# A bank for products of ones, and the order of the first loads, in an attention and feed-forward block

## The chip, the cores and the metric

The kernel runs on one core of a Trainium2 chip. The metric is the device time of one execution in microseconds (us); the time before the change is the median of three runs.

## The reference

The input x has 2048 rows (tokens) of 512 numbers. Two branches are computed from it and joined:

```python
x = A_x
xn = _layernorm(x, axis=-1)
s = _A_ref(xn, A_wqkv, A_wo)           # sliding attention, 32 heads of 16, window 256
g = _silu(_B_ref(xn, B_w1, B_w3, B_w2))  # silu(xn @ w1) * (xn @ w3) @ w2, inner width 1792
return x + s * g
```

In `_A_ref` the queries, keys and values come from one product with `wqkv` (512 x 1536). A token sees itself and the 255 tokens before it; the softmax of the scaled scores weighs the values, and the result is multiplied by `wo`. All tensors are float32.

## The kernel before

**Number format.** Nearly every matrix product is made of three float16 products. An operand is scaled by a power of two and cut into a high float16 part and a low one (`split`: ScalarE casts the high part, VectorE subtracts it for the low part; `split_pool` leaves the subtraction to GpSimd). The scale comes from the norm of each weight: `squares` sums squares on ScalarE (L249) and VectorE (L251), the sums are cast to bf16 (L261), `powers` adds them over the partitions by a product with ones (L280, or L285 inside a bank of scores), and VectorE turns the sum into a power of two (L291 to L304).

**Tiling.** Tokens go in four tiles of 512 (t = 0 to 3), heads in four groups of eight (g), and the feed-forward width in 14 blocks of 128 (f). `project(t, g, k)` makes the queries (k = 0) or keys (k = 1) of one tile and group: it accumulates twelve products (L596) in one PSUM bank, ScalarE takes the high part out (L613), VectorE the low part (L617), and both are stored to DRAM (`dQ`, `dK`, L620 to L624). `fetch(t, g)` loads them back in another layout (L640, four DMAs). `value(j)` makes the values of 128 tokens (L566, taken out in L569). `pass1` computes scores for their row maxima (L664, L678), `negate` and `finish` prepare the maxima as extra rows of the queries (L690, L691, L697, then DMAs in L708), and `pass2` computes the scores again, their exponentials (L755) and the products with the values (L773). `gate_up(t, f)` is the feed-forward's first step (L1035), `down` and a later folded form its second (L1260, L1178).

**PSUM.** Two banks m0 and m1 are handed out in turn by `bank()`. Two double banks for scores are handed out in turn by `scores_bank()`. One more, `po`, belongs to the outputs of attention.

**Loads of weights.** `load(0, f)` loads block f of w1 and w3 (two DMAs, L867), `load_down(0, f)` block f of w2 (L912), `weights_qk(g)` the query and key weights of a group (two DMAs, L394), `weights` those of the values (L358). All go through SyncE's queue (SP). Each load notes its DMA in `lasts["load"]`; so does `fetch`. `measure(f)` takes the norms of blocks f and f + 1 of w1 and w3.

**Order.** The order of TensorE's instructions is the order in which the program writes them. The other engines' instructions, and SP's DMAs, are put in an order at compile time from estimated times and from priorities; `tc.issue_after(ins)` adds that what is written inside it stands behind `ins` on the same engine. It is an order only and makes no wait by itself. Each engine then works down its list. `behind_load()` is `issue_after` the last noted load. `later(n, f)` calls f after n more steps of the program, and a step follows each piece of dense work.

**The opening.** The program loads the first tile of x, the weights of groups 0 and 1, the values' weights, blocks 0 and 1, the weights of group 2 and blocks 2 and 3 (L1508 to L1524). TensorE meanwhile runs products of ones whose results nobody reads (`keep_busy`, L1533): 24 of them at the start, 3 behind the first norm, and 4 behind the transposes (L1560). Then come the projections of tile 0, group 0 (`k00`, `q00`, L1563), those of group 1, two parts of the values, and the first scores with values and feed-forward work spread between them. The first keys are projected in a scores bank, the first queries in an m bank.

Of the kernel before, what the change touches and what calls it, by code (L numbers as in the profile page):

```python
# [10 lines left out]
F32 = mybir.dt.float32  # L11
# [10 lines left out]
P = 128  # L22
# [9 lines left out]
TW = S // NT  # L32
# [30 lines left out]
LEAD = 5  # L63
# [20 lines left out]
def tile_block(ctx: ExitStack, tc: tile.TileContext, x, wqkv, wo, w1, w3, w2, out):  # L84
    nc = tc.nc
# [18 lines left out]
    pss = pool("pss", 2, PSUM)  # L104
# [39 lines left out]
    def later(n, f):  # L144
        made_so_far[0] += 1
        queue.append((now[0] + n, made_so_far[0], f))
# [16 lines left out]
    def bank(shape, dtype=F32):  # L163

        open_bank[0] = b = 1 - open_bank[0]
        return psm.tile(shape, dtype, name=f"m{b}", tag=f"m{b}", bufs=1)

    def scores_bank():

        return pss.tile([P, 2, 512], F32, name="s")  # L170
# [65 lines left out]
    def behind_load():  # L236

        return tc.issue_after(lasts["load"].ins) if "load" in lasts else nullcontext()
# [341 lines left out]
    def project(t, g, k, terms=(range(3),), scores_bank=False):  # L580


        cell = {}

        parts = ([[(c, i) for c in (2 * half, 2 * half + 1) for i in range(3)] for half in range(2)] if len(terms) == 1
                 else [[(c, i) for i in group for c in range(NC)] for group in terms])

        def part(n):
            assert turned[t] == 4
            w = WQ[t, g, k]  # L590
            xh, xl = X[t]
            if n == 0:
                cell["pp"] = pss.tile([P, 2, TW], F32, name="s")[:, 0, :] if scores_bank else bank([P, TW])
            for c, i in parts[n]:
                a, b = ((0, xh), (1, xh), (0, xl))[i]
                nc.tensor.matmul(cell["pp"], w[:, (a * NC + c) * P:(a * NC + c + 1) * P], b[:, c, :], start=(c, i) == parts[0][0],  # L596
                                 stop=(c, i) == parts[-1][-1])
            if n < len(parts) - 1:
                return
            if t == 0:  # L600
                def store():
                    with behind_load():
                        nc.sync.dma_start(dWQ[g, k], w)
                    give(w, after=8)
                later(45, store)
            else:
                give(w)
            pp = cell["pp"]
            both = take(F16)
            B = both.rearrange("p (a t) -> p a t", a=2)  # L610
            s = QS / (XS * WS)
            with urgent():
                nc.scalar.activation(B[:, 0, :], pp, AF.Copy, scale=s)  # L613

            def rest():
                with urgent():
                    lasts["emptied"] = nc.vector.scalar_tensor_tensor(B[:, 1, :], pp, s, B[:, 0, :], op0=ALU.mult, op1=ALU.subtract)  # L617
                d = (dQ, dK)[k][g][:, :, t * TW:(t + 1) * TW]
                if k == 0:
                    nc.sync.dma_start(d[:, 0:2, :], B[:, 0:1, :].to_broadcast([P, 2, TW]))  # L620
                    nc.sync.dma_start(d[:, 2, :], B[:, 1, :])
                else:
                    nc.sync.dma_start(d[:, 0:2, :], B)
                    nc.sync.dma_start(d[:, 2, :], B[:, 0, :])  # L624
                give(both, after=4)
            later(1, rest)
        return opening([(len(l), lambda n=n: part(n)) for n, l in enumerate(parts)])
# [230 lines left out]
    def load(t, f):  # L858
        if t:
            a = [take(F16) for _ in range(2)]  # L860
            WF[t, f] = [a, None]
            for k in range(2):
                lasts["load"] = nc.sync.dma_start(a[k], dW1[f, k])
            return
        RAW[f] = raw = [take(F32) for _ in range(2)]
        for k, w in enumerate((w1, w3)):
            lasts["load"] = nc.sync.dma_start(raw[k].rearrange("p (c f) -> p c f", f=P),  # L867
                              w[:, f * P:(f + 1) * P].rearrange("(c p) f -> p c f", p=P))

    measured = set()  # L870

    def measure(f, apart=0):
# [33 lines left out]
    def load_down(t, f):  # L906
        if t:
            WF[t, f][1] = b = take(F16)
            nc.sync.dma_start(b, dW2[f])
            return  # L910
        RAW2[f] = raw = take(F32)
        lasts["load"] = nc.sync.dma_start(raw, w2[f * P:(f + 1) * P, :])  # L912

    def measure_down(k, f):

# [438 lines left out]
    def feed_forward():  # L1354

        pieces = []
        late = []
        cuts_at = []
        for t in range(NT):
            for f in range(FB):  # L1360
                if t == 0:

                    if (f % 2 or f == 0) and f + LEAD < FB - 2:
                        pieces += [(0, lambda f=f: load(0, f)) for f in (range(f + LEAD, f + LEAD + 2) if f else range(4, LEAD + 1))]
                    elif f + LEAD == FB - 1:
                        pieces += [(0, lambda f=f: load(0, f)) for f in range(FB - 2, FB)]
                    if f % 2 and f + 3 < FB:
                        pieces.append((0, lambda f=f + 3: later(5, lambda: measure(f, 1)) if f == 6 else measure(f, 1)))
                    pieces += [(0, lambda f=f: load_down(0, f)) for f in range(f + 2 if f else 0, min(f + 3, FB))]
                    for m in range(f + 1 if f else 0, min(f + 2, FB)):  # L1370
                        k = next(k for k, (_, f1) in enumerate(GROUPS) if m < f1)
                        pieces.append((0, lambda k=k, m=m: later(2, lambda: measure_down(k, m))))
                else:
                    if f == 0:
                        pieces += [(0, lambda t=t, f=f: load(t, f)) for f in range(2)]
                    if f + 2 < FB:
                        pieces.append((0, lambda t=t, f=f + 2: load(t, f)))

                    if t == 1:
                        pieces.append((0, lambda t=t, f=f: load_down(t, f)))  # L1380
                    if t == 1 and f in FOLD_AT:
                        work = fold_weights(FOLD_AT.index(f))
                        pieces.append((0, work[0]))
                        cuts_at.append((f + 2, work))
                    for at, work in cuts_at:
                        if t == 1 and f == at:
                            pieces.append((0, work[1]))
                if f == FB - 4 and t + 2 < NT:
                    first, second = prepare_beside(t + 2, 8)
                    pieces += first  # L1390
                if f == 0 and t > 2:
                    pieces += soon
                made = gate_up(t, f)
                for at, work in cuts_at:
                    if t == 1 and f == at:
                        made.insert(2, (0, lambda work=work: later(6, work[2])))
                pieces += made
                pieces += late
                late = []
                if t < 2:  # L1400
                    for k, (f0, f1) in enumerate(GROUPS):
                        if f == f1 - 1:
                            late = [q for b in range(4) for q in down(t, k, b)]
                for k, (j0, j1) in enumerate(FOLDS):
                    if t > 1 and f == 2 * j1 - 1:
                        soon, late = folds(t, k)
                        if k == 0 or t == NT - 1:
                            pieces += soon
            if t + 2 < NT:
                pieces.append((0, second))  # L1410
        return pieces + late
# [85 lines left out]
    def run(dense):  # L1497
        for c, piece in dense:
            piece()
            if c:  # L1500
                step()
# [18 lines left out]
    load(0, 0)  # L1520
    load(0, 1)
    qk[2][0]()
    load(0, 2)
    load(0, 3)  # L1524

    for b in range(VB):
        nc.gpsimd.memset(V[:, b, 0:H * VW].rearrange("p (h w) -> p h w", w=VW)[:, :, DH:VW], 1.0)
# [2 lines left out]
        nc.gpsimd.memset(KA[2][:, a, :].bitcast(F32), TWO_ONES)  # L1530


    def keep_busy(n):  # L1533
        ps = bank([P, 4, P])
        for _ in range(n):
            nc.tensor.matmul(ps, onesb, onesb.unsqueeze(1).to_broadcast([P, 4, P]), start=True, stop=True)

# [19 lines left out]
        flush()  # L1557
    with tc.issue_after(lasts["hi"].ins), tc.issue_after(lasts["x"].ins):
        qk[1][1]()
    keep_busy(4)  # L1560


    k00, q00 = (project(0, 0, k, ((0,), (1,), (2,)), k) for k in (1, 0))  # L1563
    run([k00[0], q00[0], k00[1]])
    qk[1][2]()
    with tc.issue_after(lasts["scale"].ins):
# [3 lines left out]
    with tc.issue_after(lasts["hi"].ins):  # L1570
        run([k00[2], q00[2]])
    later(1, lambda: fetch(0, 0))
    k01 = project(0, 1, 1, ((0, 2), (1,)))
    run(k01[:1])
    wv[2]()
# [4 lines left out]
    sc["o"] = scaled(SQ["wv"][3], OS / WS, "so")  # L1580
    with tc.issue_after(lasts["hi"].ins):
        measure(0)
    run(project(0, 1, 0, scores_bank=True))
    later(1, lambda: fetch(0, 1))
    run(value(0, True))
    qk[2][1]()
    run(value(1))
    qk[3][0]()
    started.append(True)
    measure(2, 1)  # L1590
    beside_scores(4, lambda s: then(s, qk[2][2](s), lambda: later(1, qk[2][3])))
# [84 lines left out]
```

## Time and profile before

| what | value |
|---|---|
| median of three runs | 813.16 us (813.06 to 813.75) |
| the profiled execution | 813.03 us |
| its span, from the first to the last instruction | 811.2 us |
| TensorE busy | 794.5 us, 98% of the span |
| VectorE, ScalarE, GpSimd busy | 634.2, 392.5 and 364.0 us |
| granted TensorE clock | 1.000 |
| moved by DMA | 134.18 MB, mean 165 GB/s |

In the profile PE is TensorE, PEld its weight loads, DVE VectorE, ACT ScalarE, POOL GpSimd, and SPq stands for DMAs as SyncE issues them. A row of a timeline gives the start in us, the length in us, the engine, the line of the kernel, the operation, what it writes and reads, and how often; in square brackets stands how long the engine had been idle and what it waited for. A row of the waits gives who waited for whom, the total in us, how many times, and the longest. A row of the windows gives for a stretch of time the length, the busy time and count of each engine, the granted clock, the share of the time that the 16 DMA engines were busy, and GB/s.

### The profile page before, as it was taken

To read this page: it belongs to the slowest core of one execution; us is meant where nothing else is said; L and a number is where in the kernel's file an instruction comes from. 1 tells how busy PE (TensorE), PEld (TensorE's weight loads), DVE (VectorE), ACT (ScalarE), POOL (GpSimd) and SP (SyncE) were. 2 spreads that over 40 slices of the span, in tenths; PEclk is the share of its full clock that TensorE was granted. 3 is DMA by queue.
4 is the path that set the end of the run, shared out by engine and by line. 5 is a ranking of instruction groups with operands and counts; after the bars stand their busy time and mean duration, and the time that the engine had idled before them with its cause. 6 is when DMAs were issued, how large, how long until landed. Compare 5 with 4: busy or idle time off the path is not lost.

```text
span 811.2 us, 23867 instructions
## 1 busy us (share of the span) xinstructions
PE 794.5 (98%) x9176; PEld 404.2 (50%) x9176; DVE 634.2 (78%) x2037; ACT 392.5 (48%) x591; POOL 364.0 (45%) x648
## 2 busy tenths in 40 slices
PE   8999989999999999999999999999999999999998
PEld 4444444444544444444444454456544654466465
DVE  8788788887898777887988888777777887875437
ACT  6879586563536554445444434344444234344421
POOL 2234266232329546354354355530246277560670
PEclk9999999999999999999999999999999999999999
DMA  9978554835566375657655634656462544335321
GB/s 283 253 221 264 156 190 124 283 117 190 158 180 215 127 249 140 214 145 251 171 162 175 193 98 132 174 150 176 116 189 72 162 138 139 113 85 174 112 67 60
DMA packets 109794, 134.18 MB, mean 165 GB/s; under 512 B 18864, under 2 KB 64880, under 8 KB 109680
## 3 DMA queue, kind: packets, MB, share of 16 engines
q1 hardware_dynamic: 109392, 132.13, 54.7%
q8 instruction: 72, 1.18, 0.6%
q10 hardware_dynamic: 288, 0.52, 0.2%
q14 instruction: 42, 0.34, 0.1%
HBM read 91.23 MB, written 36.57 MB: 158 GB/s over the span
## 4 chain that ended last, share of the span: by engine, by line
PE 80%; DVE 9%; ACT 5%; issue 3%; DMA 2%; SPq 0%; DVEq 0%; POOL 0%; ACTq 0%
PE m L1035 30%; PE po L773 8%; PE m L1260 8%; PE m L1178 8%; PE m L596 7%; PE s L745 5%; PE m L1312 4%; PE m L566 4%; PE s L664 3%; DVE junk L678 2%; PE po L664 2%; ACT sqa L249 1%; ACT slot L342 1%; ACT pt L755 1%; DMA dW<-slot 1%
## 5 line engine op out<-in xcount | busy, mean ns | idle before, releaser
L1035 PE MATMUL m<-XH,slot 128*128 128x512 f16 x896 | 267.3, 380 | 1.6 <-DVE slot L617 1.2
L755 ACT ACTIVATE pt<-s,es 128x1024 f32<-128x1024 f32 x152 | 167.7, 1113 | 192.8 <-DVE s L752 174.6
L339 POOL TENSOR_TENSOR slot<-slot,slot 128x256 f16<-128x256 f32 (+1 forms) x170 | 113.2, 694 | 212.2 <-ACT slot L1068 85.0
L1035 PEld LDWEIGHTS <-slot 128*128 128x128 f16 x1344 | 124.8, 98 | 155.9 <-issue 12.4
L1035 PE MATMUL m<-XL,slot 128*128 128x512 f16 x448 | 169.8, 379 | 0.0
L752 DVE TENSOR_TENSOR s<-s,MK 128x256 f32<-128x256 f32 (+2 forms) x280 | 118.8, 435 | 50.7 <-PE s L745 46.4
L678 DVE CUSTOM_DVE_ANT_0 junk<-s,MW 128x320 bf16<-128x320 f32 x276 | 133.9, 485 | 18.0 <-PE s L664 10.3
L678 DVE CUSTOM_DVE_ANT_0 junk<-po,MW 128x320 bf16<-128x320 f32 x172 | 83.5, 485 | 4.3
L1260 PE MATMUL m<-slot,slot 128*128 128x512 f16 x336 | 78.6, 380 | 0.4 <-DVE slot L1054 0.4
L773 PE MATMUL po<-pt,V 64*32 64x320 f32 (+4 forms) x2880 | 77.2, 342 | 0.8 <-DVE pp L304 0.8
L596 PE MATMUL m<-XH,slot 128*128 128x512 f16 x240 | 70.9, 380 | 1.5 <-DVE slot L1054 0.8
L1178 PE MATMUL m<-slot,slot 128*128 128x256 f16 x588 | 68.4, 273 | 0.0
L1093 POOL TENSOR_TENSOR slot<-slot,slot 128x256 f16<-128x256 f32 x98 | 64.6, 671 | 1.1
L1050 ACT ACTIVATE slot<-m,sgs 128x512 f32<-128x512 f32 x56 | 38.3, 684 | 54.4 <-PE m L1035 53.0
L1178 PEld LDWEIGHTS <-slot 128*128 128x128 f16 x588 | 56.2, 98 | 11.4 <-issue 3.0
L773 PEld LDWEIGHTS po<-pt,V 64*32 64x32 f32 x2880 | 50.4, 106 | 23.0 <-PE s L514 0.9
L1054 DVE SCALAR_TENSOR_TENSOR slot<-slot,m 128x512 f32<-128x512 f32 x56 | 38.3, 684 | 27.9 <-ACT slot L1050 27.8
L745 PE MATMUL s<-qa,KA 50*64 50x320 f16 (+3 forms) x1472 | 58.3, 259 | 0.3 <-DVE M L678 0.2
L596 PEld LDWEIGHTS <-slot 128*128 128x128 f16 x384 | 35.6, 98 | 44.7 <-issue 3.3
L745 PEld LDWEIGHTS <-KA 50*64 50x64 f16 x1472 | 30.1, 105 | 52.1 <-issue 31.4
L1260 PEld LDWEIGHTS <-slot 128*128 128x128 f16 x336 | 30.7, 98 | 38.7 <-issue 4.3
L664 PE MATMUL s<-KA,qa 48*64 48x320 f16 (+3 forms) x824 | 45.0, 294 | 4.1 <-ACT pt L755 2.9
(188 smaller groups left out, 1096.9 us busy)
## 6 DMA issues: line engine op xcount, KB each, us to landing
slot<-dW SPq DMA_DIRECT2D x98, 256.0 KB
slot<-in_B_w_dram SPq DMA_DIRECT2D x56, 256.0 KB
slot<-dFold SPq DMA_DIRECT2D x48, 256.0 KB
dW<-slot SPq DMA_DIRECT2D x42, 256.0 KB
slot<-in_A_x_dram SPq DMA_DIRECT2D x30, 256.0 KB
KA<-dK SPq DMA_DIRECT2D x24, 288.0 KB
qa<-dQ SPq DMA_DIRECT2D x32, 192.0 KB
slot<-dWQ SPq DMA_DIRECT2D x24, 256.0 KB
```

Source lines behind the costliest of these rows:

```text
L339: op(out[:, c], a[:, c], b[:, c])
L596: nc.tensor.matmul(cell["pp"], w[:, (a * NC + c) * P:(a * NC + c + 1) * P], b[:, c, :], start=(c, i) == parts[0][0], stop=(c, i) == parts[ ...
L664: nc.tensor.matmul(s[c:c + w, r, :n], qa[rows, 2 * p + a, ii * P + c:ii * P + c + w], ka[rows, 2 * p + a, e - n:e], start=True, stop=True)
L678: lasts["maximum"] = nc.vector.tensor_tensor_reduce(out=junk[:, :n], in0=s[:, r, :n], in1=mask, scale=1.0, scalar=NEG, op0=ALU.add, op1=AL ...
L745: nc.tensor.matmul(s[64 * h:64 * h + 64, r, o:o + 64 * n], ka[rows, 2 * p + a, 64 * (m + 4):64 * (m + 5)], qa[rows, 2 * p + a, 64 * (m + k ...
L752: nc.vector.tensor_add(v, v, MK[:, kind, of:of + n, :].unsqueeze(1).to_broadcast([P, 2 * len(which), n, 64]))
L755: lasts["exp"] = nc.scalar.activation(pt, s, AF.Exp, scale=es)
L773: nc.tensor.matmul(cell["po"][32 * i:32 * i + 32, h, 64 * (m + k):64 * (m + k + n)], V[64 * h:64 * h + 64, (4 * t + m // 2) % VB, hd * VW: ...
L1035: nc.tensor.matmul(cell[k], w[:, (a * NC + c) * P:(a * NC + c + 1) * P], b[:, c, :], start=c == 0 and i == 0, stop=c == NC - 1 and i == 2)
L1093: nc.gpsimd.tensor_sub(lo, view, hi)
L1178: nc.tensor.matmul(cell["ps"][:, c], made[:, f:f + P], wj[:, g:g + 256], start=j == j0 and c == 0 and n == 0, stop=j == j1 - 1 and n == 2, ...
L1260: nc.tensor.matmul(ps, hh[:, a * TW + b * P:a * TW + (b + 1) * P], w[:, c * D:(c + 1) * D], start=f == f0 and i == 0, stop=f == f1 - 1 and ...
```

## The change

Three things are changed. The second group of products of ones is written to a scores bank, the one in which the first keys are then projected, and has three products instead of four; the first queries stay in an m bank. The loads of feed-forward blocks 2 and 3 leave the opening list and are written one step behind the first `fetch`, and they, like the later loads of w1 and w3 of tile 0 up to block 11, and like those of w2, stand behind the load noted last. The weights of the last query and key group (`qk[3]`) also stand behind the load noted last, which there is the second fetch. `project` now takes the function `scores_bank` or False instead of a flag.

```diff
@@ project
-                cell["pp"] = pss.tile([P, 2, TW], F32, name="s")[:, 0, :] if scores_bank else bank([P, TW])
+                cell["pp"] = bank([P, TW]) if scores_bank is False else scores_bank()[:, 0, :]
@@ after load
+    def load_behind(t, f):
+        with behind_load():
+            load(t, f)
@@ load_down
-        lasts["load"] = nc.sync.dma_start(raw, w2[f * P:(f + 1) * P, :])
+        with behind_load():
+            lasts["load"] = nc.sync.dma_start(raw, w2[f * P:(f + 1) * P, :])
@@ feed_forward
-                        pieces += [(0, lambda f=f: load(0, f)) for f in (range(f + LEAD, f + LEAD + 2) if f else range(4, LEAD + 1))]
+                        pieces += [(0, lambda f=f: load_behind(0, f)) for f in (range(f + LEAD, f + LEAD + 2) if f else range(4, LEAD + 1))]
@@ the opening
     load(0, 1)
     qk[2][0]()
-    load(0, 2)
-    load(0, 3)
...
-    def keep_busy(n):
-        ps = bank([P, 4, P])
+    def keep_busy(n, ps=None):
+        ps = bank([P, 4, P]) if ps is None else ps
...
-    keep_busy(4)
-
-
-    k00, q00 = (project(0, 0, k, ((0,), (1,), (2,)), k) for k in (1, 0))
+    waiting = scores_bank()
+    keep_busy(3, waiting[:, 0, :].rearrange("p (k q) -> p k q", q=P))
+
+
+    k00, q00 = (project(0, 0, k, ((0,), (1,), (2,)), (lambda: waiting) if k else False) for k in (1, 0))
...
     later(1, lambda: fetch(0, 0))
+
+    def loads():
+        for f in (2, 3):
+            load_behind(0, f)
+    later(1, loads)
     k01 = project(0, 1, 1, ((0, 2), (1,)))
...
-    run(project(0, 1, 0, scores_bank=True))
+    run(project(0, 1, 0, scores_bank=scores_bank))
...
-    qk[3][0]()
+    with behind_load():
+        qk[3][0]()
```

## Prediction

> **What bounds the kernel now.** I read the page's head first, then the busy time of each engine in four stretches, then what TensorE (PE) waited for, then the timelines of single queues.
>
> ```profile
> span 811.2 us, 23867 instructions
> PE 794.5 (98%) x9176; PEld 404.2 (50%) x9176; DVE 634.2 (78%) x2037; ACT 392.5 (48%) x591; POOL 364.0 (45%) x648
> ```
>
> ```profile
> core 0: us, PE busy (x) PEld busy (x) DVE busy (x) ACT busy (x) POOL busy (x), PEclk, DMA share, GB/s
> 0.00:45.00 45.00, 41.91 (x232) 19.12 (x232) 36.72 (x128) 33.11 (x65) 11.29 (x41) 1.00 1.01 276
> 45.00:200.00 155.00, 145.99 (x1578) 69.01 (x1584) 128.80 (x487) 104.08 (x189) 66.77 (x118) 1.00 0.60 190
> 200.00:700.00 500.00, 499.61 (x6191) 251.10 (x6171) 400.12 (x1255) 216.67 (x284) 236.11 (x405) 1.00 0.55 161
> 700.00:811.20 111.20, 106.95 (x1195) 64.96 (x1192) 68.52 (x172) 38.62 (x53) 49.83 (x85) 1.00 0.34 104
> ```
>
> PE is idle for 811.2 - 794.5 = 16.7 us in all. From 200 to 700 us it loses 0.4 us: there nothing but PE's own work counts. The change edits the opening, where PE loses 45.00 - 41.91 = 3.1 us, and it can reach the next stretch, where PE loses 9.0 us, only through what is late or early when that stretch begins. The last stretch loses 4.3 us and is out of reach. The DMA share of 1.01 in the first 45 us says that the transfer engines are full there, and only there.
>
> ```profile
> engine line waited for: us in total, times, longest us
> PE s L664 <- ACT pt L755: 2.9, 3, 1.6
> PE m L1035 <- DVE slot L617: 1.2, 2, 1.0
> PE s L664 <- DMA qa<-dQ: 0.9, 2, 0.6
> PE m L1536 <- DVE XL L500: 0.6, 1, 0.6
> ```
>
> These are PE's waits before 200 us that matter here. The last two are what the change aims its two edits at; together they are 1.5 us. The first two belong to the stretch from 45 us on and are waits for vector and scalar work, not for data.
>
> **Products of ones.** The second group of products of ones writes bank m1, which DVE still reads (L500, first block of tokens). In the changed kernel it writes a scores bank, which has no reader left, and there are three products instead of four.
>
> ```profile
> 11.62 0.60 PE L492 MATMUL s<-identf,slot 128*128 128x128 f32 x4
> 12.80 1.02 PE L1536 MATMUL m<-onesb 128*128 128x512 bf16 x4 [0.58 <-DVE XL L500]
> 13.66 1.03 PE L596 MATMUL s<-XH,slot 128*128 128x512 f16 x4
> 16.25 0.19 PE L280 MATMUL s<-sb,onesb 128*128 128x1 bf16 x2
> ```
>
> ```profile
> 12.37 0.62 ACT L495 CAST XH<-s 128x512 f16<-128x512 f32 x1
> 15.62 0.17 DVE L261 CAST sb<-ssq 128x2 bf16<-128x2 f32 x1
> ```
>
> Four products take 13.66 - 12.80 = 0.86 us, so one is 0.215 us. After the change three of them follow the transposes directly: 11.62 + 0.60 = 12.22, plus 0.65 is 12.87. The first projection then needs the last part of XH, which ACT finishes at 12.37 + 0.62 = 12.99; I take 13.05 with the signal. That is 13.66 - 13.05 = 0.61 us earlier, with 0.18 us of new idle time in front of it. Three projection parts later stand the norm products of L280, now at 16.25. They would be reached at 16.25 - 0.61 = 15.64, but their operand sb is cast by DVE until 15.62 + 0.17 = 15.79, and that cast is the product of scalar squares that the change doesn't touch. So L280 runs at about 15.88, and of the 0.61 us only about **0.37 us** are left. From there the chain runs through it (scale of the second weights, their cuts, the next projection, the scale of the value weights), so the 0.37 us go on to the scalar work at 22.64, below. Bounds of this term: 0 (if DVE's order moves the cast back by as much) and 0.61.
>
> **Loads of blocks 2 and 3.** They are four DMAs on SP that now stand ahead of the stores of the first keys and queries. After the change they stand behind the four loads of the first fetch.
>
> ```profile
> 14.41 2.65 SPq L867 DMA_DIRECT2D slot<-in_B_w_dram  x4
> 21.04 0.43 SPq L621 DMA_DIRECT2D dQ<-slot  x1
> 21.53 1.26 SPq L394 DMA_DIRECT2D slot<-in_A_wqkv_dram  x1
> 24.64 0.82 SPq L640 DMA_DIRECT2D KA<-dK  x2
> 25.55 0.88 SPq L640 DMA_DIRECT2D qa<-dQ  x2
> 31.10 0.81 SPq L640 DMA_DIRECT2D KA<-dK  x2
> ```
>
> ```profile
> 29.80 0.24 PE L664 MATMUL s<-KA,qa 48*64 48x128 f16 x1 [0.28 <-DMA qa<-dQ]
> 30.67 0.30 PE L664 MATMUL s<-KA,qa 48*64 48x128 f16 x7 [0.63 <-DMA qa<-dQ]
> ```
>
> ```profile
> slot<-in_B_w_dram SPq DMA_DIRECT2D x56, 256.0 KB
> qa<-dQ SPq DMA_DIRECT2D x32, 192.0 KB
> KA<-dK SPq DMA_DIRECT2D x8, 192.0 KB
> ```
>
> ```profile
> 15.00:20.00 5.00, 5.00 (x27) 2.28 (x26) 4.24 (x16) 3.85 (x8) 0.00 (x0) 1.00 1.17 290
> 20.00:25.00 5.00, 5.00 (x28) 2.33 (x27) 4.95 (x16) 2.96 (x5) 0.00 (x0) 1.00 0.85 263
> 30.00:35.00 5.00, 4.37 (x30) 1.88 (x30) 3.92 (x19) 5.00 (x11) 2.26 (x3) 1.00 1.04 285
> ```
>
> The four loads are 4 x 256 KB = 1.05 MB, at 290 GB/s 3.6 us of a full queue, in front of the stores that the fetch waits for. The first fetch is 4 x 192 KB = 0.79 MB, 2.7 us. Without the four loads, and without the load of the last query and key weights (L394 at 21.53, 1.26 us of SP), the fetch can start when the stores have landed. The last store leaves SP at 21.04 + 0.43 - 0.37 = 21.1; now the fetch follows it by 24.64 - 21.47 = 3.2 us with the full queue in between, and I take half of that, an estimate: 22.6 us against 24.64, two us earlier. PE reaches the first scores at 29.80 - 0.28 - 0.37 = 29.15; the queries, issued by about 24.3, have nearly five us to land, where now the last ones take from 25.55 to 30.67. So **both waits, 0.28 + 0.63 = 0.91 us, go**. Bounds: 0 to 0.91; I take the upper end, since two us more is twice what is missing.
>
> The price of the move is at the other end. The four loads are issued from about 24.3 and need 22.6 + (0.79 + 1.05) / 0.29 = 28.9 us to be through. Their first reader is the measure of blocks 2 and 3:
>
> ```profile
> 28.88 0.63 ACT L249 ACTIVATE sqa<-slot 128x512 bf16<-128x512 f32 x1
> 35.93 0.62 ACT L249 ACTIVATE sqa<-slot 128x512 bf16<-128x512 f32 x1
> 36.67 0.63 ACT L249 ACTIVATE sqa<-slot 128x512 bf16<-128x512 f32 x1
> ```
>
> The row at 28.88 squares w1 of block 2, which is the first of the four loads and through at about 26.2 us; block 3's w1, the third, is through at 28.0 and wanted 0.7 us after 28.5. The cover is 1 to 2 us, so I cost the delay at **nothing**; without that cover each us is a us of ACT, which has no gap there (5.00 of 5.00 us busy from 30 to 35). The stores of the second keys and queries now queue behind those loads, and the second fetch (31.10) may slip by up to 1 us; nothing reads it before the second group of heads.
>
> **The last query and key weights, and later loads in a row.** Both loads of `qk[3]` move behind the second fetch, from 21.53 and 28 us to 33 us. The rows at 35.93 and 36.67 read them. By bytes: 31.1 + (0.79 + 0.52) / 0.285 = 35.7 us for both (285 GB/s from the row of 30 to 35 us). Against a wanted 35.6 and 36.3 that is about even: I cost it at nothing, with ends of -0.4 (ACT works ahead) and +1.5 us (the fetch slips as well). The later feed-forward loads and those of w2 only get an order that they already have: SP issues them in program order from 33 us on. That is nothing.
>
> **The sum.** 0.37 + 0.91 = 1.28 us off the profiled execution's 813.03 us (span 811.2 and 1.83 around it), so 811.75; the median of the runs is 813.16, 0.13 above, so **811.9 us**. The removed product is inside the 0.61 and not counted again. What is late next:
>
> ```profile
> 22.64 1.95 ACT L333 ACTIVATE wvh<-slot,swwv 128x512 f16<-128x512 f32 x3 [0.26 <-DVE swwv L302]
> 37.43 0.68 DVE L261 CAST sb<-ssq 128x2 bf16<-128x2 f32 x1 [0.33 <-ACT sqa L249]
> 45.39 0.18 DVE L691 SCALAR_TENSOR_TENSOR NM<-M,NM 128x16 f16<-128x16 f32 x1
> 45.62 0.22 PE L697 MATMUL s<-identh,NM 64*64 64x64 f16 x2
> ```
>
> PE's L697 stands directly behind DVE's NM (45.39 + 0.18 = 45.57), and DVE's work before it hangs on the cast at 37.43, which waits for ACT. So the lead is kept whole at 45 us only if DVE too has used its earlier scores; otherwise it shrinks to ACT's 0.37 us.
>
> **The rivals.**
> *More than the sum.* Orders of ACT and DVE are made from estimated times, and earlier scores can pull some of the 9.0 us of PE idle time after 45 us together, above all the 1.0 us behind L617 and the 2.9 us behind L755. For it: DVE has idle time around 30 us that earlier scores fill. One or two of these waits on top, 1 to 2.5 us: 809.4 to 810.9.
> *Slower: the moved loads arrive late.* ACT and DVE run their lists in order, so a square that waits for `qk[3]` (35.93) or for block 2 holds the value eviction behind it, the cast at 37.43, NM at 45.39 and PE's L697. It decides as soon as the second fetch slips by more than about 1.5 us past 31.1, or the loads of blocks 2 and 3 are through after 30. Price: 2 to 3.5 us of delay at 45 us, less the 0.37 gained, so +1.6 to +3.1: 814.8 to 816.3. Against it: the byte sums above, which come out even, not late. The Trainium skill's "DMA: Bandwidth & Descriptors", Rules for kernel authors, speaks for this rival: it says to issue a DMA early and to wait for it late. The trace bears it out half: ACT never waits for these weights now, but the queries behind them do wait.
> *The lead is lost.* PE waits at L697 for what it gained, and a small wait moves in behind: 812.8 to 813.5.
>
> **How the numbers follow.** 0.2% of 813.16 is 1.6 us, about what a measurement of this kernel can tell from no change. The forecast, 810.9 to 812.7, has a chance of 0.43, of which 0.20 lies below 811.5. More than the sum: 0.18. Loads late: 0.29, with 0.27 beyond 814.8. Lead lost: 0.10. Faster is 0.20 + 0.18 = 0.38, same 0.23 + 0.10 + 0.02 = 0.35, slower 0.27. The range leaves out the outer end of the two outer cases: 809.6 to 815.4. Within it the forecast's own range is 810.9 to 812.7.
>
> **What would show it.** Right: PE's wait for XL L500 and both waits for qa<-dQ are gone, the first L596 starts near 13.05 and L280 near 15.9, the first fetch is issued near 22.6, and PE idles about 2.0 us up to 45 us instead of 3.1. Wrong: ACT's L249 rows waiting for a DMA of in_B_w or in_A_wqkv between 28 and 38 us; L697 waiting for NM; or PE's idle time from 45 to 200 us away from 9.0 by more than 1 us in either direction.

## The result and the profile after

The changed kernel takes 817.18 us (median of 6 runs, 816.75 to 818.69), the kernel before 813.12 us beside it: a ratio of 1.0052, 95% interval 1.0042 to 1.0062. It is slower by 4.1 us. The profiled execution took 817.04 us. The changed file has a few lines more: before's L1005, L1006, L1035 and L1323 are L1010, L1011, L1040 and L1328 here, and lines up to L867 keep their numbers.

The page's head after, and the same four stretches as before:

```profile
span 815.3 us, 23880 instructions
PE 794.2 (97%) x9175; PEld 403.8 (50%) x9175; DVE 633.2 (78%) x2037; ACT 392.6 (48%) x591; POOL 364.3 (45%) x648
```

```profile
0.00:45.00 45.00, 41.91 (x230) 18.91 (x231) 36.58 (x135) 32.83 (x63) 10.93 (x41) 1.00 0.89 240
45.00:200.00 155.00, 145.44 (x1589) 69.08 (x1591) 128.06 (x481) 104.53 (x192) 66.51 (x118) 1.00 0.60 193
200.00:700.00 500.00, 495.84 (x6150) 249.00 (x6135) 396.96 (x1245) 214.30 (x281) 232.98 (x399) 1.00 0.54 163
700.00:815.30 115.30, 111.01 (x1228) 66.79 (x1226) 71.58 (x180) 40.92 (x57) 53.84 (x91) 1.00 0.35 104
```

PE's idle time, length less busy, stretch by stretch, before and after: 3.09 and 3.09, 9.01 and 9.56, 0.39 and 4.16, 4.25 and 4.29. The opening that was edited is even. The loss of 3.8 us lies between 200 and 700 us, where PE had lost only 0.39 us and where no edited line runs any more: the last load that the edits touch is issued at 154 us.

PE's waits after, and the two places of the first of them:

```profile
PE m L596 <- DMA slot<-dWQ: 3.5, 2, 2.5
PE s L664 <- ACT pt L755: 2.8, 3, 1.6
PE s L285 <- DVE sb L931: 2.0, 1, 2.0
PE s L664 <- DMA qa<-dQ: 1.3, 2, 0.9
```

```profile
315.33 0.41 PE L745 MATMUL s<-qa,KA 50*64 50x256 f16 x8
342.58 0.60 PE L596 MATMUL m<-XH,slot 128*128 128x512 f16 x2 [2.48 <-DMA slot<-dWQ]
388.84 0.60 PE L596 MATMUL m<-XH,slot 128*128 128x512 f16 x2 [0.97 <-DMA slot<-dWQ]
```

The same two instructions of the kernel before:

```profile
315.29 0.41 PE L745 MATMUL s<-qa,KA 50*64 50x256 f16 x8
339.90 0.59 PE L596 MATMUL m<-XH,slot 128*128 128x512 f16 x2
```

At 315 us the changed kernel is 0.04 us behind; at the next projection of a later tile it is 2.68 behind, of which 2.48 is one wait for the projection's weights (`load_qk`, L631, which fetches the cut weights from `dWQ`). The wait of 2.0 for sb at 106.55 looks large too, but the milestone at 315 shows that it had been made up for.

Why are the weights late? SP's queue after, then before, with the stores of the output (L1328 after, L1323 before):

```profile
339.12 0.34 SPq L1328 DMA_DIRECT2D out_dram<-slot  x1
339.50 0.43 SPq L631 DMA_DIRECT2D slot<-dWQ  x1
...
385.57 0.34 SPq L1328 DMA_DIRECT2D out_dram<-slot  x1
386.01 0.38 SPq L631 DMA_DIRECT2D slot<-dWQ  x1
```

```profile
334.39 0.34 SPq L1323 DMA_DIRECT2D out_dram<-slot  x1
334.77 1.33 SPq L631 DMA_DIRECT2D slot<-dWQ  x1
...
375.32 0.60 SPq L631 DMA_DIRECT2D slot<-dWQ  x1
...
382.19 0.34 SPq L1323 DMA_DIRECT2D out_dram<-slot  x1
```

At the first place the load stands behind a store in both kernels, but the store leaves 4.73 us later. At the second place the load stood 6.9 us ahead of the store and now stands behind it. From issue to the reader's start a load takes 342.58 - 339.50 = 3.1 and 388.84 - 386.01 = 2.8 us; issued at 334.77 it has 5.1 us, so two us of slack covered it. And why is the store late? GpSimd adds the residual, and the store writes out the sum. L339 is a helper's line that other work uses too; in the row of 336.41 the last two of the four are the add (337.67 to 339.09, just ahead of the store), in the row of before both are. GpSimd's list after, and one row of before:

```profile
333.20 0.68 POOL L1011 TENSOR_TENSOR slot<-slot,slot 128x256 f16<-128x256 f32 x1 [2.13 <-ACT slot L1007]
333.82 0.74 POOL L1010 CAST slot<-slot 128x256 f16<-128x256 f32 x2
334.52 1.94 POOL L1011 TENSOR_TENSOR slot<-slot,slot 128x256 f16<-128x256 f32 x3
336.41 2.68 POOL L339 TENSOR_TENSOR slot<-slot,slot 128x256 f16<-128x256 f32 x4
```

```profile
332.94 1.43 POOL L339 TENSOR_TENSOR slot<-slot,slot 128x256 f32<-128x256 f32 x2
```

SP's longest wait for that add between 290 and 392 us, after and before:

```profile
SPq L1328 <- POOL slot L339: 19.2, 4, 9.1
SPq L1323 <- POOL slot L339: 13.7, 4, 4.4
```

The add is queued behind cuts of the second feed-forward weights, which wait for ScalarE; SP stands 9.1 us at the first of the two stores with everything behind it. All of this is a matter of order: the compile-time planner, given other loads in the opening, made other lists far beyond it. In a line diff of the lists as the traces have them (operation, source line, tiles), 114 of SP's 933 transfers stand elsewhere than before, the last at 465 us, with 43 of ScalarE's 596 instructions (the last at 131 us) and 19 of GpSimd's 665 (the last at 386 us).

### The profile page after: what moved, and what is told of

It is laid out like the page before. It is cut to its first block, busy times and chain, and to the rows that moved or that the text cites. A ratio compares the mean times of both kernels' runs of the same rounds, so it can differ in the third digit from the quotient of the medians.

```text
span 815.3 us, 23880 instructions
## 1 busy us (share of the span) xinstructions
PE 794.2 (97%) x9175; PEld 403.8 (50%) x9175; DVE 633.2 (78%) x2037; ACT 392.6 (48%) x591; POOL 364.3 (45%) x648
## 4 chain that ended last, share of the span: by engine, by line
PE 79%; DVE 9%; DMA 4%; ACT 3%; issue 2%; POOL 2%; SPq 1%; DVEq 0%; ACTq 0%; POOLq 0%
PE m L1040 30%; PE po L773 8%; PE m L1183 8%; PE m L596 7%; PE m L1265 7%; PE s L745 5%; PE m L566 4%; PE m L1317 4%; PE s L664 3%; DVE junk L678 2%; PE po L664 2%; PE m L1539 1%; DVE s L752 1%; DMA dW<-slot 1%; DMA dK<-slot 1%
## 5 line engine op out<-in xcount | busy, mean ns | idle before, releaser
L1040 PE MATMUL m<-XH,slot 128*128 128x512 f16 x896 | 267.3, 380 | 1.6 <-DVE slot L617 1.2
L339 POOL TENSOR_TENSOR slot<-slot,slot 128x256 f16<-128x256 f32 (+1 forms) x170 | 112.4, 689 | 212.8 <-ACT slot L1073 68.9
L1040 PEld LDWEIGHTS <-slot 128*128 128x128 f16 x1344 | 125.0, 98 | 155.5 <-issue 12.8
L1040 PE MATMUL m<-XL,slot 128*128 128x512 f16 x448 | 169.8, 379 | 0.0
L596 PE MATMUL m<-XH,slot 128*128 128x512 f16 x240 | 70.9, 380 | 4.4 <-DMA slot<-dWQ 3.5
L773 PEld LDWEIGHTS po<-pt,V 64*32 64x32 f32 x2880 | 50.4, 106 | 22.6 <-issue 0.8
L596 PEld LDWEIGHTS <-slot 128*128 128x128 f16 x384 | 35.5, 98 | 48.5 <-DMA slot<-dWQ 4.4
```

Source lines behind the costliest of these rows:

```text
L339: op(out[:, c], a[:, c], b[:, c])
L773: nc.tensor.matmul(cell["po"][32 * i:32 * i + 32, h, 64 * (m + k):64 * (m + k + n)], V[64 * h:64 * h + 64, (4 * t + m // 2) % VB, hd * VW: ...
L1040: nc.tensor.matmul(cell[k], w[:, (a * NC + c) * P:(a * NC + c + 1) * P], b[:, c, :], start=c == 0 and i == 0, stop=c == NC - 1 and i == 2)
```

## The experiments

Two theories. **F, the far order**: the load part of the change makes the planner put the loads of `dWQ` behind late output stores, and the waits at 342.58 and 388.84 us are the loss. **O, the opening**: the prediction's own slower rival, loads of blocks 2 and 3 and of `qk[3]` that arrive late. For O speak ScalarE's waits: 0.37 us for a load of block 2 or 3 at 33.41 and

```profile
42.07 0.63 ACT L249 ACTIVATE sqa<-slot 128x512 bf16<-128x512 f32 x1 [1.49 <-DMA slot<-in_A_wqkv_dram]
```

**e1_bank: the bank for the products of ones alone.**

```diff
-    keep_busy(4)
+    waiting = scores_bank()
+    keep_busy(3, waiting[:, 0, :].rearrange("p (k q) -> p k q", q=P))
... all loads as in the kernel before
```

> Only the bank part: products of ones in the scores bank, three of them, loads as before. Theory F (far order: the time was lost where the order of GpSimd and SP around 330 to 390 us changed, with loads of dWQ behind a late store of the output): the dWQ load that PE waited for at 388.84 stands ahead of that store here and the residual additions are not behind the fold's subtractions, so no wait for dWQ; 812.6 to 813.4 us. Theory O (opening: the later loads hold up ACT and DVE and PE pays later): no load is later here, so 812.7, the 0.4 us of the earlier L280. Both: PE's wait for XL L500 gone, L280 at about 15.9 to 16.1.

Measured: 812.86 us against 813.18, ratio 0.9998 (0.9989 to 1.0007). No wait for `dWQ`. In the opening PE gains and later gives it back:

```profile
0.00:45.00 45.00, 42.34 (x231) 19.01 (x231) 37.12 (x134) 33.01 (x64) 11.30 (x41) 1.00 0.99 273
45.00:200.00 155.00, 145.85 (x1590) 69.36 (x1592) 128.66 (x482) 104.10 (x191) 67.03 (x118) 1.00 0.60 189
200.00:700.00 500.00, 499.03 (x6178) 250.73 (x6162) 399.61 (x1253) 216.51 (x284) 235.75 (x405) 1.00 0.56 162
```

Idle time to 45 us is 2.66 instead of 3.09, from 45 to 200 us 9.15 instead of 9.01, from 200 to 700 us 0.97 instead of 0.39. The bank part does no measurable good and no harm; the loss is in the loads.

**e2_loads: the load part alone** (products of ones as before, moved loads and loads in a row as in the change).

```diff
-    waiting = scores_bank()
-    keep_busy(3, waiting[:, 0, :].rearrange("p (k q) -> p k q", q=P))
+    keep_busy(4)
... against the changed kernel; its loads are kept
```

> Only the load part (blocks 2 and 3 behind the first fetch, qk[3] behind the second, later loads in a row); products as before. On every engine but PE the order is the same as in the changed kernel. F: 817 to 817.7 us, both waits for dWQ there (about 2.5 and 1.0 us). O: the same time, since the loads are the cause there too; but if the four added waits of ACT for loads before 50 us were what costs, PE would be late by the time it reaches 300 us. F says PE is within 0.3 us of before at 318 us.

Measured: 817.88 us, ratio 1.0053 (1.0041 to 1.0066): the whole loss.

```profile
314.76 0.41 PE L745 MATMUL s<-qa,KA 50*64 50x256 f16 x8
...
341.89 1.03 PE L596 MATMUL m<-XH,slot 128*128 128x512 f16 x2 [2.35 <-DMA slot<-dWQ]
```

At 315 us this kernel is 0.53 us ahead of before, although ScalarE waits for the moved weights here too (0.64 us at 40.98); the loss comes behind that. F had allowed 0.3 us at that point and 817.7 us at most, so its sizes are a little off, but what O needs, a PE that is late by then, isn't there.

**e3_no_row: the change without "in a row"** for the later loads (bank, blocks 2 and 3 and `qk[3]` moved).

```diff
-        with behind_load():
-            lasts["load"] = nc.sync.dma_start(raw, w2[f * P:(f + 1) * P, :])
+        lasts["load"] = nc.sync.dma_start(raw, w2[f * P:(f + 1) * P, :])
...
-  lambda f=f: load_behind(0, f)
+  lambda f=f: load(0, f)
```

> The change without the later loads in a row: blocks 4 and 5 then take the freed places ahead of the first stores, so the queue is as full there as before, and the order from 330 us on is that of e1_bank. F: 812.6 to 813.6 us, no wait for dWQ. O: blocks 2 and 3 and qk[3] are as late as in the changed kernel, so 815 to 817.

Measured: 813.0 us, ratio 1.0 (0.9991 to 1.0009), no wait for `dWQ`, PE busy 499.24 of the 500 us from 200 to 700. Its first weights of a later tile leave SP in time, as before:

```profile
334.96 0.34 SPq L1327 DMA_DIRECT2D out_dram<-slot  x1
335.35 1.55 SPq L631 DMA_DIRECT2D slot<-dWQ  x1
```

So the moved loads and the row do harm together only. The row by itself, put into the kernel before, leaves every engine's list as it was, so it was not run. Without the row the planner fills the freed places with the loads of blocks 4 and 5. Which of the moved loads the harm needs beside the row, blocks 2 and 3 or `qk[3]`, was not separated.

**e4_dwq_first: the whole change, and the loads of `dWQ` urgent for the planner.**

```diff
-        nc.sync.dma_start(w, dWQ[g, k])
+        with urgent():
+            nc.sync.dma_start(w, dWQ[g, k])
```

> The changed kernel with one edit: the loads of dWQ (L631) get the higher priority that stores to the queries have, so that they stand ahead of the output's store in SP's list at both places. Orders of PE, DVE and ACT are those of the changed kernel, the opening is untouched. F: both waits go, 3.45 us: 817.2 - 3.45 = 813.7 us, 813.2 to 814.3. O: 816.5 to 817.5.

Measured: 813.32 us, ratio 1.0002 (0.9993 to 1.0011). Lines behind L631 are one higher here; L632 is the load.

```profile
313.33 0.38 SPq L632 DMA_DIRECT2D slot<-dWQ  x1
...
339.87 0.34 SPq L1329 DMA_DIRECT2D out_dram<-slot  x1
```

```profile
340.70 0.59 PE L596 MATMUL m<-XH,slot 128*128 128x512 f16 x2
```

```profile
41.72 0.63 ACT L249 ACTIVATE sqa<-slot 128x512 bf16<-128x512 f32 x1 [1.46 <-DMA slot<-in_A_wqkv_dram]
```

This run tells the two apart best. The store is as late as in the changed kernel (339.87), ScalarE still waits 1.46 us for the moved weights, and PE's 2.0 us at sb are still there; of the waits that set the changed kernel apart only the ones for `dWQ` are gone, as the load no longer stands behind the store, and with them the 4 us. (SP's list differs from the changed kernel's in other places, too, by 135 of 933 transfers; ScalarE's and VectorE's are the same. A run that moves the two loads alone was not made.) F holds, O falls: a late store costs nothing by itself, a load that someone needs behind it does.

**e5_before_dwq: the same edit in the kernel before**, as a control (the diff of e4).

> Control for the run before: the kernel before with nothing but the load of dWQ (L631) made urgent. The far-order theory says that this load is the place of the loss only where it stands behind an output store, which is not so in the kernel before: 813.2, ratio 0.999 to 1.001, and PE's busy time from 300 to 400 us stays near 99.9. Then all of the 4 us that the urgent load won back in the changed kernel was lost at that load. The rival, that the urgent load is worth something by itself and only covers a loss of the same size elsewhere: 1.5 us or more below the kernel before, 811.7 or less.

Measured: 813.17 us against 813.26, ratio 1.0001 (0.9992 to 1.001), PE busy 99.93 us from 300 to 400. The edit has no gain of its own that could have covered another loss in e4.

**e6_extra_loads: what the first stores and the first fetch wait for.**

```diff
+    spare = [take(F32) for _ in range(4)]
+    for i, raw in enumerate(spare):
+        nc.sync.dma_start(raw, wo[i * P:(i + 1) * P, :])
+    give(*spare)
```

> The kernel before with four more loads of 256 KB (parts of wo that nobody reads) behind the loads of blocks 2 and 3, so in front of the first stores. It leaves nothing out and adds 1.05 MB to the queue. My prediction took the time from the first stores to the first fetch for a queue full of loads: by that the fetch (24.64 now) is issued at 24.64 + 3.6 = about 28.2, and PE loses 3 us or more at the first scores, 816 or more. The rival: stores and fetch do not stand behind the bytes already issued, and the distance is the stores' own time of about 4 us; then the fetch stays within 0.7 us of 24.6, the queries land at most 1 us later, and the time is 813 to 814.5.

Measured: 816.11 us, ratio 1.0034 (1.0024 to 1.0043); the profiled execution, 814.49 us, is the shortest of its ten. The fetch and the first scores:

```profile
26.51 0.81 SPq L640 DMA_DIRECT2D KA<-dK  x2
```

```profile
31.63 0.24 PE L664 MATMUL s<-KA,qa 48*64 48x128 f16 x1 [1.81 <-DMA qa<-dQ]
```

Neither expectation is right on the fetch, though the median falls into the first one's time, 816 or more. The fetch slips by 26.51 - 24.64 = 1.9 us, not by 3.6 and not by under 0.7, of which some 0.3 us come from the execution itself (products of ones start at 13.10 instead of 12.80). One more store, of the second keys at 23.59, also stands ahead of the fetch here. So bytes ahead of the stores do count, but by less than their own time. What the other runs of this kernel lost beyond the profiled 1.5 us is open. The next section puts four kernels side by side.

**e7_bank_dwq: the bank part with the urgent load of `dWQ`, no load moved** (the diffs of e1 and e4).

> The bank for the products of ones, with the urgent load of dWQ and no load moved: the part of the change that is free of harm, with the far order held. The opening gains 0.4 us at L280 and PE has 0.4 us less idle time by 45 us. If that lead survives, 812.6 to 812.8 against 813.2; if a small later wait takes it back, as in the run with the bank alone, 813.0 to 813.3. Either way within 0.2% of the kernel before. A ratio under 0.998 would say that the order, not the bank, is worth something.

Measured: 812.89 us, ratio 0.9999 (0.999 to 1.0007). The part without harm is also without a gain that can be measured. In this trace PE's idle time to 45 us is even 3.53 us (41.47 busy), with a wait of 1.1 us at L280 for its cast, so the 0.4 us of the expectation wasn't there. No version here beats the kernel before.

## Why the prediction was wrong, point by point

811.9 us was forecast, 809.6 to 815.4 as the range; 817.18 came.

**Later loads in a row: "That is nothing".** This step failed, and with it the total. It was judged by SP's order in one trace, as if only the lines that the diff touches could move. Together with the moved loads the row changed SP's list up to 465 us, and the two loads of `dWQ` cost 2.48 + 0.97 = 3.45 of the 4.1 us. No rival held it: the two that lose time placed the loss at or before 45 us, and the prediction said that the change reaches the next stretch "only through what is late or early when that stretch begins". Where a planner makes the lists there is this second way, and the range had no room for it. The stretch from 200 to 700 us, with 0.39 us of idle time, was read as safe; it was in fact the stretch with the most to lose.

**Products of ones: 0.37 us at L280.** Right in the opening.

```profile
11.90 0.60 PE L492 MATMUL s<-identf,slot 128*128 128x128 f32 x4
12.34 0.81 PE L1539 MATMUL s<-onesb 128*128 128x512 bf16 x3
13.31 1.02 PE L596 MATMUL s<-XH,slot 128*128 128x512 f16 x4 [0.16 <-ACT XH L495]
...
16.11 0.20 PE L280 MATMUL s<-sb,onesb 128*128 128x1 bf16 x2
```

In this execution x came 0.28 us later (11.90 against 11.62). Against that the first L596 is 0.35 + 0.28 = 0.63 us earlier (0.61 forecast), the new wait 0.16 (0.18), and L280 0.42 us earlier (0.37). But e1 shows that it doesn't reach the end: the total is the same within 0.1%. The rival "the lead is lost", at 0.10, comes nearest for this part, though the lead went in small waits behind 200 us and not at L697.

**Both waits for the queries go, 0.91 us.** Failed. They became 0.40 + 0.86 = 1.26 us:

```profile
20.32 0.36 SPq L623 DMA_DIRECT2D dK<-slot  x1
20.91 0.33 SPq L621 DMA_DIRECT2D dQ<-slot  x1
22.28 0.33 SPq L624 DMA_DIRECT2D dK<-slot  x1
24.52 0.81 SPq L640 DMA_DIRECT2D KA<-dK  x2
25.44 0.87 SPq L640 DMA_DIRECT2D qa<-dQ  x2
26.36 2.09 SPq L867 DMA_DIRECT2D slot<-in_B_w_dram  x4
```

```profile
22.00:24.00 2.00, 2.00 (x11) 0.87 (x9) 1.95 (x10) 1.74 (x4) 0.00 (x0) 1.00 0.43 138
24.00:26.00 2.00, 2.00 (x11) 0.88 (x10) 2.00 (x4) 2.00 (x5) 0.00 (x0) 1.00 0.17 51
```

The step took half away of "3.2 us with the full queue in between". The fetch went at 24.52, not 22.6, though the transfer engines were nearly empty (share 0.43 and 0.17). The stretch of 20 to 25 us, with its mean of 0.85, had hidden that they are half empty there in the kernel before, too:

```profile
22.00:24.00 2.00, 2.00 (x11) 0.92 (x10) 1.95 (x9) 1.74 (x4) 0.00 (x0) 1.00 0.58 190
```

What the fetch waited for stands in the traces' records of landings. Each of these stores reports 16 parts, as many as there are transfer engines, and the fetch is issued within 0.1 us of the last part of the first keys (times in us; the store is the one whose last part comes last):

| kernel | store issued | 15th part in | 16th part in | fetch issued | packet of instructions |
|---|---|---|---|---|---|
| before | 20.44 | 23.62 | 24.56 | 24.64 | 21.35 to 22.42 |
| changed | 20.32 | 22.52 | 24.51 | 24.52 | 22.12 to 23.43 |
| e2_loads | 20.45 | 23.36 | 23.36 | 23.38 | 20.17 to 21.18 |
| e6_extra_loads | 21.17 | 25.93 | 26.44 | 26.51 | 23.52 to 24.62 |

So the step was right in kind and failed at the last part. Taking the four loads away brought 15 of the 16 parts in 1.1 us earlier, at 22.52, so that the fetch could have gone when the forecast had it (a store of the second keys, at 22.28, stands ahead of it on SP); the 16th came 2.0 us behind them and gave it all back. What held it up is most likely the last column: in each trace one packet of 16 KB of instructions is moved here, in 0.9 to 1.5 us. In eight of the nine traces it begins while this store is under way, and the store's last part comes 0.5 to 2.0 us behind the 15th. In e2 it ends before the bytes of the store begin to move (22.0 us), and all 16 parts land together; so the fetch goes at 23.38 there, 1.1 us earlier than with the same list in the changed kernel, and no wait for the queries is left. The records don't name the engine that a part or a packet ran on, and no run moved this packet, so this cause is read from the times and not shown.

**Delay of blocks 2 and 3 and of `qk[3]`: nothing.** Right in cost, wrong in reason. The byte sums promised the loads in time; they weren't, and the rival's sign appeared (ScalarE waiting at 33.41 and 42.07). But the planner had moved the squares of `qk[3]` from 35.93 to 42.07, later in ScalarE's list, and NM came earlier, at 44.43 instead of 45.39:

```profile
44.43 0.18 DVE L691 SCALAR_TENSOR_TENSOR NM<-M,NM 128x16 f16<-128x16 f32 x1
```

Later loads did not hold up a list that had been made for later loads. For the same reason the slower rival, "the moved loads arrive late", is not what happened, although its time of 814.8 to 816.3 is the nearest.

**What would show it.** XL's wait at L500 is gone, as said; the waits for the queries are not; PE's idle time to 45 us is 3.09, not 2.0; from 45 to 200 us it is 0.55 us above before, inside the 1 us that was allowed. One sign of being wrong did appear, ScalarE waiting for a load of in_B_w at 33.41, by 0.37 us; all the signs named lie in the first 200 us, and none of them shows the loss.

## What to carry to other kernels

Where engines' lists are made by a planner, an edit of order can be an edit of every list, far beyond the lines it touches: compare the lists line by line, and price first the stretch that has no idle time. Look in them for a DMA that an engine needs soon and that stands behind one whose own wait is late; e4 repaired it with one priority. And before a queue is blamed for a distance between a store and its reader, look at the share of the transfer engines in steps as short as that distance, and at when each part of the store landed.

## What was not expected of the hardware

A store to DRAM of 256 KB holds its reader for 4.2 us in the changed kernel (20.32 to 24.52) and 2.9 us in e2, with a near empty queue: the reader waits for the slowest of 16 parts. The view of the bytes shows the part that is late:

```profile
GB/s 62 15 179 358 333 328 354 338 348 333 420 287 31 0 0 97 333 195 10 10 20 26 20 5 0 0 0 61 87 292 358 379 297 225 205 149 102 92 164 256
```

This is the window of 20 to 28 us of the changed kernel in 40 slices of 0.2 us. The first stores end at the 13th slice, and the short burst at 23.0 is the store issued at 22.28. From 23.6 to 24.8 only 5 to 26 GB/s move, of 330 to 360 with all engines at work, which fits one engine of 16 with the late parts of three stores. The fetch begins to move at 25.4.

The Trainium skill's "DMA: Bandwidth & Descriptors", section Anatomy of one DMA, written for transfers that GpSimd issues, says that a fixed cost of about 2.0 us is mostly the receipt for the last byte, heaviest to HBM. These stores, issued by SyncE, don't show that: 15 parts of the store issued at 22.28 end their bytes between 23.46 and 23.62 and report between 23.78 and 23.99, some 0.35 us later. The section also says that a semaphore is waited for on the issuing sequencer before dispatch; SP's 9.1 us at the output store, with the load of `dWQ` behind it, agree with that.
